# Sort products of the second head pair as two halves of 64 rows, in eights, batched with score units

## The chip, the cores and the metric

The kernel runs on one core of a Trainium2 chip. The core has a matrix engine (TensorE, "PE" in the profile, with its weight loads as "PEld"), a vector engine (VectorE, "DVE"), a scalar engine (ScalarE, "ACT"), a general one (GpSimd, "POOL") and a sync engine that issues DMAs (SyncE, "SP"). The metric is the device time of one execution in microseconds; before the change it was 233.67 (median of three runs, 233.46 to 234.27).

## The reference, cut to what matters

A block-sorted attention over 4 batches, 8 heads, 768 positions and a head dimension of 64, followed by a layer of a mixture-of-experts kind without routing:

```python
P = sort_net                                  # (B, H, 8, 8), five Sinkhorn rounds
k_sorted = einsum('bhij,bhjcd->bhicd', P, k_b)   # blocks of 96 positions, mixed by P
v_sorted = einsum('bhij,bhjcd->bhicd', P, v_b)
scores = scale * q_b @ k_sorted.T             # within each block of 96
attn = softmax(scores)
x = (attn @ v_sorted) as (3072, 512)
h = x @ w_in                                  # 512 -> 2048
out = (h * cos(h)) @ w_out                    # 2048 -> 512
```

## The kernel before

**Staging.** The 3072 rows of the result are worked through in eight *chunks* `n` of 384 rows; chunk `n` is half of batch `n // 2`. A chunk has four *units* `u` of 96 positions (one sorted block) with all 8 heads. For each unit come scores (TensorE into PSUM), maximum and subtraction (VectorE, lines 489 and 491; chunks 0 and 1 lines 781 and 785), an exponential (ScalarE, line 533), a transpose of the weights (by a DMA from the sync queue, line 551, or on TensorE, line 568), `av` (TensorE, line 588), the normalization (VectorE, lines 599 and 601) and a transpose of the result into `xT[n]` (DMA, line 607, or TensorE, line 619). Then the chunk goes through the up layer (line 632: eight steps of eight matmuls of 384 columns, each with a cosine on ScalarE and a product on VectorE) and the down layer (line 657: six half-tiles of eight matmuls of 512 columns).

**Order.** It is written out by hand: engines run their instructions in the order in which the program emits them. `moe_up` and `moe_down` take lists of calls that are emitted between their steps (`slots`) or in the middle of a half-tile (`mid`, `late`). So work of the next chunks (scores, sort products, `av`) stands between the matmuls of the present chunk. The end of the list (from line 1092) is where chunk 1's down layer, chunk 2's up and down layers and so on stand.

**Sort products.** Keys and values are mixed by `P` on TensorE, for a pair of batches at once: the contraction runs over 128 rows, which are 2 batches x 8 heads x 8 blocks, and the moving matrix `bds[1]` (128 x 128) is block-diagonal: rows 0 to 63 (batch 2) have values in columns 0 to 63 only, rows 64 to 127 (batch 3) in columns 64 to 127 only. `k_sort_g` (line 411) does four keys products and copies their 512 columns out with one instruction on ScalarE; `v_sort_g` (line 456) does four or eight values products. 48 key products (`t` from 0) go to `kT2`, 64 value products (`d` from 0) to `vS[1]`. `k_next` and `w_next` take the next four; `w_two` takes eight. After the last key product two DMAs (`k_swap`) exchange halves of the sorted keys.

**Scores.** `scores` (line 436) multiplies 128 rows, of which the 64 of the other head of a pair are zeros in `q_turned`; a unit is 8 such matmuls of 96 columns. `qk_two` (line 498) does two units with the 64 rows that matter alone; the two heads of a pair take different halves of the rows and different PSUM banks. It is used twice, for units (2,2), (2,3) and (5,0), (5,1). `s_ps` (line 754) does units of chunks 0 and 1, chunk 0's in 64 rows by another path (line 764).

**PSUM.** Two pools of slots: `big`, three slots of two banks, and `acc`, two slots of one bank. A tile waits until the last reader of its slot is done.

Of the kernel before, what the change touches and what calls it, by code (L numbers as in the profile page):

```python
# [10 lines left out]
FP32 = mybir.dt.float32  # L11
# [7 lines left out]
def kernel(  # L19
# [112 lines left out]
    def q_of(n, e):  # L132
        return q_turned[n % 2][:, e]
# [277 lines left out]
    def k_sort_g(t0, eng, pool, tag):  # L411
        ps = pool.tile([128, 4, 4 * NB], FP32, name="ks", tag=tag)
        for t in range(4):
            k_products(ps, t, t0 + t, slice(0, 128), bds[1].rearrange("p x i -> p (x i)"),
                       pair)
        copy_on(
            eng, kT2[:, ::2, :, :, t0:t0 + 4].rearrange("p e b m t -> p b e m t"),
            ps.rearrange("p t (b e m) -> p b e m t", b=2, e=2))
# [9 lines left out]
    def keys_of(n, u, h2, hp):  # L428
        g, b2, ih = where(n)
        z = slice(hp, hp + 2)  # L430
        m = h2 * nb + ih * IC + u
        if n < 2:
            return kT[0][:, z, m]
        return kT[1][:, z, m] if g == 0 else kT2[:, z, b2, m]
# [6 lines left out]
    def v_cols(d, permuted, m=128):  # L441
        return vperm[:, d * blk:d * blk + m] if permuted else vv[:, d]
# [13 lines left out]
    def v_sort_g(d0, nd, eng, pool, tag):  # L456
        ps = pool.tile([128, nd, 4 * NB], FP32, name="vs", tag=tag)
        for t in range(nd):
            m = 128 if t < nd - 1 else blk
            nc.tensor.matmul(  # L460
                ps[:m, t], v_cols(d0 + t, True, m), bds[1].rearrange("p x i -> p (x i)"),
                start=True, stop=True)
        copy_on(eng, vS[1][:, :, d0:d0 + nd], ps[:blk].rearrange("p t n -> p n t"))
# [21 lines left out]
    def qk_reduce(n, u, part, sc):  # L485
        w = len(part)
        scv = sc[:blk].rearrange("p e (h c) -> p (e h) c", c=128)[:, :, :blk]
        mx = small.tile([blk, w * H2], FP32, name="mx", tag="mx")
        nc.vector.reduce_max(mx[:], scv, axis=AX.X)  # L489
        s = s_t[n, u][:, part[0]:part[0] + w].rearrange("p e h c -> p (e h) c")  # L490
        nc.vector.tensor_tensor(s, scv, mx.to_broadcast(list(s.shape)), op=ALU.subtract)  # L491

    def qk(n, u):

        s_t[n, u] = sp.tile([blk, 2, H2, blk], FP32, name="s", tag="s")
        qk_part(n, u, [0, 1], big, "big")

    def qk_two(n, u0, u1):

        us = (u0, u1)  # L500
        tiles = [big.tile([128, 2, 512], FP32, name="sc", tag="big") for u in us]
        for u, sc in zip(us, tiles):
            for h2 in range(H2):
                x = (u * H2 + h2) * blk
                for hp in range(2):
                    rows = slice(hp * D, (hp + 1) * D)
                    nc.tensor.matmul(
                        sc[:, hp, h2 * 128:h2 * 128 + blk], q_of(n, hp)[rows, x:x + 128],
                        keys_of(n, u, h2, hp)[rows], start=True, stop=True)
        for u, sc in zip(us, tiles):  # L510
            s_t[n, u] = sp.tile([blk, 2, H2, blk], FP32, name="s", tag="s")
            qk_reduce(n, u, [0, 1], sc)

    def qk_av(n, u, m, *zs):

# [12 lines left out]
    def expo(n, u, on_pe=False):  # L528
        p = p_bufs[cnt[0] % NP]
        cnt[0] += 1  # L530


        nc.scalar.activation(  # L533
            p[:, :, :blk], s_t.pop((n, u)).rearrange("p e h c -> p (e h) c"), AF.Exp,
            scale=scale)
        if u == 0 and n in (NQ, NQ + 1):

            w = 2 * H2 * blk
            c = 2 * (QZ + D) + (n - NQ) * w
            t = kbuf[:, c:c + w].rearrange("p (a c) -> p a c", c=blk)  # L540
        elif n < LATE:
            t = ptp.tile([128, 2 * H2, blk], BF16, name="pT", tag="pT")
        else:

            z, w = (n * IC + u) % 8, 2 * H2 * blk
            t = vperm[:, z * w:(z + 1) * w].rearrange("p (a c) -> p a c", c=blk)
        pT[n, u] = t
        if on_pe:
            pb[n, u] = p
        else:  # L550
            nc.sync.dma_start_transpose(out=t[:], in_=p.rearrange("p a c -> p (a c)"))
# [12 lines left out]
    def p_transpose(n, u, eng, pool, tag):  # L564
        p = pb.pop((n, u))
        ps = pool.tile([128, 2 * H2, 128], BF16, name="pps", tag=tag)
        for a in range(2 * H2):
            nc.tensor.transpose(ps[:blk, a, :blk], p[:, a, :blk], ident[:blk, :blk])
        copy_on(eng, pT[n, u][:blk], ps[:blk, :, :blk])
# [82 lines left out]
    def down(n, ts, half, stores, mid=(), late=()):  # L652
        if half == 0:
            out_ps[ts] = acc.tile([128, Dm], FP32, name="o", tag="acc")
        o = out_ps[ts]
        for f in range(half * FC // 2, (half + 1) * FC // 2):
            nc.tensor.matmul(  # L657
                o[:], gt[n, f // 4][:, f % 4, ts * 128:(ts + 1) * 128], w_out_t[:, f, :],
                start=(f == 0), stop=(f == FC - 1))
            if f % (FC // 2) == FC // 4 - 1:  # L660
                step(mid)
            if f % (FC // 2) == FC // 4:
                step(late)
        if half == 0:
            return
        if stores is None:

            z = (n % 2 * 3 + ts) * 2 * Dm
            o_s = vbuf[:, z:z + 2 * Dm].bitcast(FP32)
        else:  # L670
            o_s = op.tile([128, Dm], FP32, name="o_s", tag="o_s")
        late = n > 0 and ts == TC // 128 - 1
        copy_on(V if late else A, o_s[:], o[:])
        if stores is None or stores == "held":
            kept[n, ts] = o_s
        else:
            store(n, ts, o_s, nc.sync if late else stores)
# [10 lines left out]
    def moe_down(n, slots=(), stores=nc.sync, mid={}, late=()):  # L688

        for e in range(2 * TC // 128):  # L690
            last = e == 2 * TC // 128 - 1
            down(n, e // 2, e % 2, stores, mid.get(e, ()), late if last else ())
            step(slots[e] if e < len(slots) else ())
# [60 lines left out]
    def s_ps(n, u, fill=0):  # L754
        o = ps["s", n, u] = big.tile([128, 2, 512], FP32, name="sc", tag="big")
        keep_warm(fill, o[:, 0])
        if n == 0:
            for a in range(2 * H2):
                hp, c = a // H2, (u * H2 + a % H2) * blk
                for x in range(2):  # L760
                    rows = slice(x * D, (x + 1) * D)
                    m, w = a % H2 * nb + u, HT if a % H2 == H2 - 1 else 64
                    keys = kT[0][rows, 2 * hp].rearrange("p m t -> p (m t)")
                    nc.tensor.matmul(
                        o[:, x, a * HT:a * HT + w], q_of(0, hp)[rows, c:c + 128],
                        keys[:, m * HT:m * HT + w], start=True, stop=True)
            return
        for h2 in range(H2):
            for hp in range(2):
                scores(o[:, hp, h2 * 128:h2 * 128 + blk], n, u, h2, hp)  # L770
# [77 lines left out]
        copy_on(eng, o_s[:], out_ps[ts][:])  # L848
        store(0, ts, o_s)

    wz = iter(range(0, D, 4))
    kz = iter(range(6, 12))

    def k_next():
# [1 line left out]

    def w_next(eng=A, pool=None, tag="acc"):
        v_sort_g(next(wz), 4, eng, pool or acc, tag)

    def w_two(eng=A):  # L860
        v_sort_g(next(wz), 8, eng, *B)
        next(wz)

    kp(2, *B)
    kp(0, *B)
# [226 lines left out]
    expo(2, 0)  # L1092
    expo(2, 1)
    down(1, 0, 0, nc.sync)
    qk_two(2, 2, 3)
    down(1, 0, 1, "held", mid=[(k_sort_g, 0, A, *C)])
    expo(2, 2)
    let_go(1, 0)
    k_sort_g(4, A, *B)
    down(1, 1, 0, nc.sync)  # L1100
    k_sort_g(8, A, *B)
    av(2, 0, True)
    qk(3, 0)
    k_sort_g(16, A, *B)
    expo(2, 3, True)
    down(1, 1, 1, nc.sync)
    k_sort_g(12, A, *B)
    p_hold(2, 2)
    for z in range(3, 6):
        load_pair(vbuf, vin_d, z * CD // 6, (z + 1) * CD // 6)  # L1110
    load_q(4)
    expo(3, 0)
    v_permute(slice(0, 128))
    av(2, 1, True)
    p_transpose(2, 3, A, *C)
    down(1, 2, 0, nc.sync)
    av(2, 2, True)
    x_transpose(2, 1, V, *B)
# [9 lines left out]

    expo(3, 1)
    expo(3, 2)  # L1130
    moe_down(2, [[(qk, 3, 3), (ones, 1), (w_two,)],
                 [(w_two,), (expo, 3, 3), (av, 3, 0)],
                 [(p_hold, 3, 3), (load_q, 5), (w_two,), (qk_av, 4, 0, 3, 1)],
                 [(w_two,)],
                 [(w_two,), (expo, 4, 0), (sine_next,)]],
             mid={3: [(av, 3, 2, True)], 4: [(av, 3, 3, True)], 5: [(x_transpose, 3, 2, V, *B, 3)]})
    q_transpose_dma(5)
    hold(q_turned[1])
# [4 lines left out]
               [(qk_half, 4, 2, 1)], [(qk, 4, 3)]])  # L1143
    expo(4, 1)
    expo(4, 2)
    moe_down(3, [[(expo, 4, 3), (av, 4, 0)], [(qk_two, 5, 0, 1)], [],
                 [(expo, 5, 0)],
                 [(av, 4, 3, True), (expo, 5, 1), (sine_next,)]],
             None, mid={3: [(av, 4, 1)], 4: [(av, 4, 2, True)]},
# [71 lines left out]
```

## Time and profile before

| | us |
|---|---|
| median of three runs | 233.67 |
| the profiled execution | 233.72 |
| its span, first to last instruction | 231.7 |
| TensorE busy | 224.7 |
| VectorE busy | 170.8 |
| ScalarE busy | 154.4 |
| GpSimd busy | 95.9 |

The stages that the diff touches, by the start of their first matmul of the up or down layer: chunk 1's units at 39.4, chunk 1's down layer from 70.2 to 85.3, chunk 2's down layer from 97.9 to 112.7.

How to read it: a line of the timeline has the start, the time from there to the end of the last instruction of the group, the engine, the line of the program and the tiles (output, then inputs), the shape and the count. TensorE's matmuls are pipelined, so the groups overlap by the length of a pipeline; the distance from one group's start to the next one's is what the group holds the engine for. A wait that stands in a view under "PEld" is the wait of a weight load, which may lie beside a matmul that still runs.

### The profile page before, as it was taken

How to read it: one execution, taken by the hardware profiler on the slowest of the kernel's cores; microseconds unless marked ns; L12 is line 12 of the kernel's file. 1: busy time of each engine (PE TensorE's matmuls, PEld its weight loads, DVE VectorE, ACT ScalarE, POOL GpSimd, SP SyncE). 2: the span in 40 equal slices, each digit the busy share in tenths (PEclk: the TensorE clock that was granted, in tenths of full speed). 3: DMA queues.
4: the chain of work that ended last, by engine and by line, in shares of the span. 5: the costliest groups of instructions: out<-in, count | busy, mean ns of one | idle time of the engine just before them, and what ended most of it. 6: DMA issues, size and time to landing. Idle time of an engine off the chain costs nothing.

```text
span 231.7 us, 5423 instructions
## 1 busy us (share of the span) xinstructions
PE 224.7 (97%) x2212; PEld 141.4 (61%) x2212; DVE 170.8 (74%) x291; ACT 154.4 (67%) x209; POOL 95.9 (41%) x121
## 2 busy tenths in 40 slices
PE   8889999999999999999999999999999999999994
PEld 3478899567665666656666456555665566556553
DVE  6769967978789857876489986997699769745700
ACT  5659877767789758795788566746675666716521
POOL 7999999399950186962708101800000000000000
PEclk9999999999999999999999999999999999999999
DMA  5999999994999899878979949954923450351012
GB/s 68 233 188 207 203 207 232 200 222 141 123 134 178 129 170 157 152 171 132 136 134 103 122 79 164 205 83 91 197 101 68 84 173 0 71 143 45 3 45 91
DMA packets 67672, 31.19 MB, mean 135 GB/s; under 512 B 56384, under 2 KB 63168, under 8 KB 67392
## 3 DMA queue, kind: packets, MB, share of 16 engines
q0 software_dynamic: 24048, 13.64, 43.5%
q1 hardware_dynamic: 43312, 17.02, 35.6%
q8 instruction: 17, 0.28, 0.5%
q10 hardware_dynamic: 288, 0.20, 0.3%
q14 instruction: 7, 0.06, 0.1%
HBM read 27.27 MB, written 6.29 MB: 145 GB/s over the span
## 4 chain that ended last, share of the span: by engine, by line
PE 85%; DVE 6%; POOL 2%; DMA 2%; ACT 1%; issue 1%; SPq 0%; POOLq 0%; ACTq 0%
PE h L632 30%; PE o L657 29%; PE h L817 5%; PE o L838 4%; PE sc L438 4%; PE av L588 3%; PE ks L408 2%; DVE s L785 2%; PE vs L460 2%; DVE mx L781 2%; PE o L1185 2%; DMA kTs<-kTs 1%; POOL w_in_t L160 1%; DMA P<-in_sort_net_dram 1%; PE xps L619 1%
## 5 line engine op out<-in xcount | busy, mean ns | idle before, releaser
L632 PE MATMUL h<-xT,w_in_t 128*128 128x384 bf16 x448 | 78.4, 326 | 0.0
L657 PE MATMUL o<-w_out_t,gg 128*128 128x512 bf16 x320 | 76.3, 379 | 0.0
L640 DVE TENSOR_TENSOR gg<-c,h 128x768 bf16<-128x768 f32 x56 | 52.7, 949 | 19.7 <-ACT c L636 19.7
L636 ACT ACTIVATE c<-h,half_pi 128x768 f32<-128x768 f32 x56 | 50.4, 900 | 25.1 <-PE h L632 24.2
L632 PEld LDWEIGHTS <-w_in_t 128*128 128x128 bf16 x448 | 42.3, 98 | 26.3 <-DVE xT L259 0.3
L657 PEld LDWEIGHTS <-gg 128*128 128x128 bf16 x320 | 29.0, 99 | 28.0
L533 ACT ACTIVATE p_buf<-s 96x768 bf16<-96x768 f32 x32 | 26.6, 842 | 5.3 <-DVE s L491 4.0
L179 POOL COPY vperm<-kv 64x768 bf16<-64x768 bf16 (+2 forms) x12 | 28.4, 2422 | 4.1 <-DMA kv<-in_v_dram 4.1
L491 DVE TENSOR_TENSOR s<-sc,mx 96x384 f32<-96x384 f32 (+1 forms) x33 | 24.3, 736 | 1.6
L489 DVE TENSOR_REDUCE mx<-sc 96x4 f32<-96x384 f32 (+1 forms) x33 | 24.0, 728 | 0.0
L601 DVE TENSOR_TENSOR xn<-av,r 96x512 bf16<-96x512 f32 x32 | 22.0, 687 | 1.1
L129 POOL DMA_DIRECT2D kv<-in_q_dram x24 | 16.0, 681 | 0.8 <-issue 0.5
L257 ACT CAST kTs<-ks 128x512 bf16<-128x512 f32 x20 | 11.3, 582 | 5.9 <-PE ks L408 5.0
L257 ACT COPY kv<-o 128x512 f32<-128x512 f32 (+2 forms) x10 | 5.2, 523 | 14.1 <-PE o L657 11.5
L599 DVE RECIPROCAL r<-av 96x8 f32<-96x8 f32 x32 | 6.4, 199 | 10.5 <-PE av L588 9.9
L438 PE MATMUL sc<-kTs,q_turned 128*128 128x96 bf16 x192 | 13.4, 206 | 0.3 <-DMA kTs<-kTs 0.3
L438 PEld LDWEIGHTS <-q_turned 128*128 128x128 bf16 x192 | 10.9, 98 | 3.2 <-issue 0.4
L129 POOL DMA_DIRECT2D q_mem<-in_q_dram x16 | 10.7, 689 | 2.9 <-DMA kv<-in_v_dram 2.5
L838 PE MATMUL o<-w_out_t,gg 128*128 128x512 bf16 x48 | 11.7, 379 | 0.0
L259 DVE COPY kv<-o 128x512 f32<-128x512 f32 (+1 forms) x5 | 3.1, 612 | 11.1 <-PE o L1185 8.5
L817 PE MATMUL h<-xT,w_in_t 128*128 128x192 bf16 x128 | 11.1, 246 | 0.0
L817 PEld LDWEIGHTS <-w_in_t 128*128 128x128 bf16 x128 | 10.5, 98 | 0.0
(130 smaller groups left out, 279.8 us busy)
## 6 DMA issues: line engine op xcount, KB each, us to landing
out_dram<-kv SPq DMA_DIRECT2D x12, 256.0 KB, 2.7
out_dram<-o_s SPq DMA_DIRECT2D x10, 256.0 KB, 3.4
w_in_t<-in_moe_w_in_dram POOLq DMA_DIRECT2D x4, 512.0 KB, 11.7
w_out_t<-in_moe_w_out_dram POOLq DMA_DIRECT2D x4, 512.0 KB, 12.3
kv<-in_k_dram POOLq DMA_DIRECT2D x2, 768.0 KB, 10.1
kv<-in_v_dram POOLq DMA_DIRECT2D x2, 768.0 KB, 13.1
pair<-in_k_dram POOLq DMA_DIRECT2D x2, 768.0 KB, 12.3
kv<-in_v_dram POOLq DMA_DIRECT2D x6, 256.0 KB, 6.2
```

Source lines behind the costliest of these rows:

```text
L129: nc.gpsimd.dma_start(out=q_heads[:, i, :, e], in_=src[:, ih * IC + i, :, e])
L179: nc.gpsimd.tensor_copy(dst, src)
L438: nc.tensor.matmul(out, q_of(n, hp)[:, x:x + 128], keys_of(n, u, h2, hp), start=True, stop=True)
L489: nc.vector.reduce_max(mx[:], scv, axis=AX.X)
L491: nc.vector.tensor_tensor(s, scv, mx.to_broadcast(list(s.shape)), op=ALU.subtract)
L533: nc.scalar.activation(p[:, :, :blk], s_t.pop((n, u)).rearrange("p e h c -> p (e h) c"), AF.Exp, scale=scale)
L601: nc.vector.tensor_tensor(xn.rearrange("p h e d -> p e h d"), avv[:, :, :, :D], r.to_broadcast([blk, 2, H2, D]), op=ALU.mult)
L632: nc.tensor.matmul(h[:, f2, :w], w_in_t[:, kk, f * 128:(f + 1) * 128], xT[n][:, kk], start=(kk == 0), stop=(kk == KC - 1))
L636: nc.scalar.activation(c[:], h[:, :, :w], AF.Sin, bias=half_pi[:, 0:1])
L640: nc.vector.tensor_tensor(gt[n, fp // 2][:, f:f + 2], c[:], h[:, :, :w], op=ALU.mult)
L657: nc.tensor.matmul(o[:], gt[n, f // 4][:, f % 4, ts * 128:(ts + 1) * 128], w_out_t[:, f, :], start=(f == 0), stop=(f == FC - 1))
L817: nc.tensor.matmul(o[:, part, f2 * w:(f2 + 1) * w], w_in_t[:, kk, f * 128:(f + 1) * 128], xT[0][:, kk, h * w:(h + 1) * w], start=(kk == 0) ...
```

## The change

- `qk_two` goes; `by_half` does one unit's scores in 64 rows, and `sort_eight` does eight sort products as 16 matmuls of 64 rows and 64 columns, one for each batch, into the two banks of a `big` slot. `place_eight` copies their 1024 columns out with one instruction.
- `batch` takes a list of such parts, allocates their slots, emits all their matmuls one after the other, and then their reductions and copies.
- In chunk 1's down layer the first eight key products join units (2,2) and (2,3), and the second eight join unit (3,0), behind the layer's fourth half-tile; the group of `t` from 16 and the exponential of (2,3) go into that half-tile, and the exponential of (3,0) moves behind the transposes of (2,3).
- In chunk 2's down layer the five eights of value products (`d` from 0 to 39) become such eights: with unit (3,3), alone, with unit (4,0), alone, alone. `av` of (3,1), which stood behind the products and unit (4,0), is now ahead of them.
- Units (1,0) and (1,1) are done in 64 rows. Units (5,0) and (5,1) stay in 64 rows, through `batch`.

```diff
+    def by_half(n, u, sc):
+
+        for h2 in range(H2):
+            x = (u * H2 + h2) * blk
+            for hp in range(2):
+                rows = slice(hp * D, (hp + 1) * D)
+                nc.tensor.matmul(
+                    sc[:, hp, h2 * 128:h2 * 128 + blk], q_of(n, hp)[rows, x:x + 128],
+                    keys_of(n, u, h2, hp)[rows], start=True, stop=True)
+
+    def sort_eight(kind, z, ps):
+
+        for t in range(8):
+            for b in range(2):
+                rows = slice(b * 64, (b + 1) * 64)
+                if kind == "ks":
+                    m, cols = 128, pair[rows, (z * 8 + t) * 2 * D:(z * 8 + t + 1) * 2 * D]
+                else:
+                    m = 128 if t < 7 else blk
+                    cols = v_cols(z * 8 + t, True, m)[rows]
+                nc.tensor.matmul(
+                    ps[:m, b, t * 2 * NB:(t + 1) * 2 * NB], cols,
+                    bds[1][rows, b * H:(b + 1) * H].rearrange("p x i -> p (x i)"),
+                    start=True, stop=True)
+
+    def place_eight(kind, z, ps, eng):
+        if kind == "ks":
+            copy_on(
+                eng, kT2[:, ::2, :, :, z * 8:z * 8 + 8].rearrange("p e b m t -> p b e m t"),
+                ps.rearrange("p b (t e m) -> p b e m t", t=8, e=2))
+        else:
+            copy_on(
+                eng, vS[1][:, :, z * 8:z * 8 + 8].rearrange("p (b n) d -> p b n d", b=2),
+                ps[:blk].rearrange("p b (t n) -> p b n t", t=8))
+
+    def batch(*parts, between=()):
+
+        tiles = []
+        for kind, *x in parts:
+            ps = big.tile([128, 2, 512], FP32, name=kind, tag="big")
+            tiles.append(ps)
+            if kind == "sc":
+                by_half(*x, ps)
+            else:
+                sort_eight(kind, x[0], ps)
+        step(between)
+        for (kind, *x), ps in zip(parts, tiles):
+            if kind == "sc":
+                s_t[tuple(x)] = sp.tile([blk, 2, H2, blk], FP32, name="s", tag="s")
+                qk_reduce(*x, [0, 1], ps)
+            else:
+                place_eight(kind, *x[:1], ps, x[1])
...
+        if u < 2:
+            by_half(n, u, o)
+            return
...
-    qk_two(2, 2, 3)
-    down(1, 0, 1, "held", mid=[(k_sort_g, 0, A, *C)])
+    batch(("sc", 2, 2), ("sc", 2, 3), ("ks", 0, A))
+    down(1, 0, 1, "held")
     expo(2, 2)
     let_go(1, 0)
-    k_sort_g(4, A, *B)
     down(1, 1, 0, nc.sync)
-    k_sort_g(8, A, *B)
     av(2, 0, True)
-    qk(3, 0)
-    k_sort_g(16, A, *B)
-    expo(2, 3, True)
-    down(1, 1, 1, nc.sync)
-    k_sort_g(12, A, *B)
+    down(1, 1, 1, nc.sync, mid=[(k_sort_g, 16, A, *B), (expo, 2, 3, True)])
+    batch(("sc", 3, 0), ("ks", 1, A))
...
-    expo(3, 0)
     v_permute(slice(0, 128))
     av(2, 1, True)
     p_transpose(2, 3, A, *C)
+    expo(3, 0)
     down(1, 2, 0, nc.sync)
...
-    moe_down(2, [[(qk, 3, 3), (ones, 1), (w_two,)],
-                 [(w_two,), (expo, 3, 3), (av, 3, 0)],
-                 [(p_hold, 3, 3), (load_q, 5), (w_two,), (qk_av, 4, 0, 3, 1)],
-                 [(w_two,)],
-                 [(w_two,), (expo, 4, 0), (sine_next,)]],
+    moe_down(2, [[(ones, 1), (batch, ("sc", 3, 3), ("vs", 0, A))],
+                 [(batch, ("vs", 1, A)), (expo, 3, 3), (av, 3, 0)],
+                 [(p_hold, 3, 3), (load_q, 5), (av, 3, 1),
+                  (batch, ("vs", 2, A), ("sc", 4, 0))],
+                 [(batch, ("vs", 3, A))], [(batch, ("vs", 4, A)), (expo, 4, 0), (sine_next,)]],
              mid={3: [(av, 3, 2, True)], 4: [(av, 3, 3, True)], 5: [(x_transpose, 3, 2, V, *B, 3)]})
```

More of the change, by code (lines that the diff above doesn't have):

```diff
@@ L496, in qk @@
         qk_part(n, u, [0, 1], big, "big")
[L498 to L512, printed above, removed]
+    def by_half(n, u, sc):
[6 more added lines that the diff above has]
+                    keys_of(n, u, h2, hp)[rows], start=True, stop=True)
@@ L849, in down_out @@
         store(0, ts, o_s)
-    wz = iter(range(0, D, 4))
+    wz = iter(range(40, D, 4))
     kz = iter(range(6, 12))
@@ L858, in w_next @@
         v_sort_g(next(wz), 4, eng, pool or acc, tag)
-    def w_two(eng=A):
-        v_sort_g(next(wz), 8, eng, *B)
-        next(wz)
     kp(2, *B)
@@ L1145 @@
     expo(4, 2)
-    moe_down(3, [[(expo, 4, 3), (av, 4, 0)], [(qk_two, 5, 0, 1)], [],
+    moe_down(3, [[(expo, 4, 3), (av, 4, 0)], [(batch, ("sc", 5, 0), ("sc", 5, 1))], [],
                  [(expo, 5, 0)],
```

## The prediction

> **What bounds the kernel now.** I read the page first, then TensorE's timeline through the stretches that the diff touches, then what TensorE waits for, and last the queues that feed those waits.
>
> ```profile
> span 231.7 us, 5423 instructions
> PE 224.7 (97%) x2212; PEld 141.4 (61%) x2212; DVE 170.8 (74%) x291; ACT 154.4 (67%) x209; POOL 95.9 (41%) x121
> PEclk9999999999999999999999999999999999999999
> PE 85%; DVE 6%; POOL 2%; DMA 2%; ACT 1%; issue 1%; SPq 0%; POOLq 0%; ACTq 0%
> ```
>
> TensorE sets the time: it is 85% of the chain that ended last, and its clock is full in every slice. So a matmul saved shortens the kernel, unless the time goes into a wait for VectorE or for a DMA. The profiled run took 233.72 us, 2.0 more than its span, and the runs' median is 233.67; I make the sum against 233.72. A measurement of this kernel can tell about 0.3%, 0.7 us, from no change.
>
> Busy times overlap here, so I price a group of matmuls by its own start and the start of the next group.
>
> ```profile
> 15.69 0.40 PE L764 MATMUL sc<-kTs,q_turned 64*128 64x64 bf16 x16
> 16.02 0.42 PE L745 MATMUL vs<-bdv,vperm 128*128 128x64 bf16 x8
> 39.41 0.84 PE L438 MATMUL sc<-kTs,q_turned 128*128 128x96 bf16 x16
> 40.09 0.38 PE L838 MATMUL o<-w_out_t,gg 128*128 128x512 bf16 x1
> 70.20 1.89 PE L657 MATMUL o<-w_out_t,gg 128*128 128x512 bf16 x8
> 72.02 0.51 PE L507 MATMUL sc<-kTs,q_turned 64*128 64x96 bf16 x16
> 72.47 1.04 PE L657 MATMUL o<-w_out_t,gg 128*128 128x512 bf16 x4
> 73.34 0.39 PE L408 MATMUL ks<-bd,pair 128*128 128x128 bf16 x4
> 73.57 1.03 PE L657 MATMUL o<-w_out_t,gg 128*128 128x512 bf16 x4
> ```
>
> Units in full rows: two (16 matmuls) take 40.09 - 39.41 = 0.68, so one takes 0.34. A sort product in full rows: four take 73.57 - 73.34 = 0.23, and eight of the same kind 100.37 - 99.93 = 0.44 (rows of part (c)): 0.056 each, 0.45 an eight. A 512-column matmul of the down layer: (73.34 - 72.47) / 4 = 0.216.
>
> In 64 rows, two units took 72.47 - 72.02 = 0.45, and the eight matmuls ahead took 1.82 instead of 8 x 0.216 = 1.73: the way in costs 0.10. Sixteen products of 64 columns in 64 rows (eight pairs) took 16.02 - 15.69 = 0.33, way out included. If way in and way out cost about 0.10 each, a pair of 96 columns costs (0.45 - 0.10) / 8 = 0.043 and a pair of 64 columns (0.33 - 0.10) / 8 = 0.029. So **an excursion into 64 rows costs 0.21**, a unit then 0.17 instead of 0.34, an eight of sort products 0.23 instead of 0.45.
>
> **The change part by part.** (a) *Chunk 1's first two units*, adjacent on TensorE: 0.21 + 2 x 0.17 = 0.55 for 0.68. Gain 0.13. VectorE and ScalarE have the same work; TensorE waits for neither there.
>
> (b) *First down layer (chunk 1).* The first eight of key products joins the pair of units that is in 64 rows already: it adds 0.23 and removes two groups of 0.22. Gain 0.21. Unit (3,0) with the second eight: 0.21 + 0.17 + 0.23 = 0.61 for 0.34 + 0.45. Gain 0.17. Two waits go with the old order:
>
> ```profile
> 76.60 0.42 PE L588 MATMUL av<-vS,pT 96*128 96x65 bf16 x8
> 77.00 0.50 PE L438 MATMUL sc<-kTs,q_turned 128*128 128x96 bf16 x8
> 77.44 0.38 PE L408 MATMUL ks<-bd,pair 128*128 128x128 bf16 x4
> 79.61 0.42 PE L588 MATMUL av<-vS,pT 96*128 96x65 bf16 x8
> 79.87 0.54 PE L568 MATMUL pps<-ident,p_buf 96*96 96x96 bf16 x8
> 77.91 0.94 DVE L489 TENSOR_REDUCE mx<-sc 96x8 f32<-96x768 f32 x1
> 78.96 0.95 DVE L491 TENSOR_TENSOR s<-sc,mx 96x768 f32<-96x768 f32 x1
> 80.31 0.69 DVE L601 TENSOR_TENSOR xn<-av,r 96x512 bf16<-96x512 f32 x1
> 83.77 0.69 DVE L601 TENSOR_TENSOR xn<-av,r 96x512 bf16<-96x512 f32 x1
> 84.51 0.34 PE xps L619 x4
> 85.34 0.33 PE L632 MATMUL h<-xT,w_in_t 128*128 128x384 bf16 x1
> 73.31 3.92 SPq L551 DMA_TRANSPOSE pT<-p_buf  x3
> DMA to landing us min/median/max: 3.0/4.1/4.8
> ```
>
> The av group before unit (3,0) held TensorE 0.40, the same group at 79.61 only 0.26: 0.14 of waiting for a slot. The unit took 0.44 instead of 0.34: 0.10 for the next slot. In the new order four matmuls, a group of sort products and four more stand between, so both go. TensorE alone would gain 0.13 + 0.38 + 0.24 = 0.75 up to 79.61.
>
> That is not what arrives at the end of the layer. Unit (3,0) now comes about 1.5 us later, and VectorE works in order: its maximum and subtraction (2.0 from 77.91 to the end of the subtraction with its pause), then three normalizations of about 0.92 with a copy of 0.3 between, 5.0 in all, before the last transposes, which already waited for that normalization (ends 84.46; transposes at 84.51). With TensorE at unit (3,0) from 78.5, its scores are readable at about 78.9 and the last normalization ends at 83.9 to 84.0: 0.5 earlier than now. The second of the three DMA transposes, issued at about 74.6, lands 3.0 to 4.8 later, 77.6 to 79.4, and its av now wants it at 79.0: if it is late, 0.3 more is lost. So I take **0.45 at the end of this layer**, chunk 1's 0.13 included (bounds 0.25 and 0.75). ScalarE's copies of 1024 columns, 1.02 each by the rows of part (c), replace two of half the size; the first delays unit (2,2)'s exponential by half of that, 0.5, so that its transpose, issued at about 75.9 now, lands at 79.4 to 81.2, and it is wanted at 81.5. The exponential of (3,0) moves behind that of the transposed copy; its DMA is read 20 us later, at 102.55. On SP's and POOL's queues nothing else changes place.
>
> (c) *Second down layer (chunk 2).*
>
> ```profile
> 99.59 0.50 PE L438 MATMUL sc<-kTs,q_turned 128*128 128x96 bf16 x8
> 99.93 0.61 PE L460 MATMUL vs<-bd,vperm 128*128 128x128 bf16 x8
> 100.37 1.89 PE L657 MATMUL o<-w_out_t,gg 128*128 128x512 bf16 x8
> 102.55 0.42 PE L588 MATMUL av<-vS,kv 96*128 96x65 bf16 x8
> 102.80 1.89 PE L657 MATMUL o<-w_out_t,gg 128*128 128x512 bf16 x8
> 104.98 0.50 PE L438 MATMUL sc<-kTs,q_turned 128*128 128x96 bf16 x8
> 105.32 0.42 PE L588 MATMUL av<-vS,pT 96*128 96x65 bf16 x8
> 105.58 1.03 PE L657 MATMUL o<-w_out_t,gg 128*128 128x512 bf16 x4
> 106.59 0.43 PE L588 MATMUL av<-vS,pT 96*128 96x65 bf16 x8
> PEld L588 <- DMA pT<-p_buf: 0.5, 1, 0.5
> 101.14 2.56 SPq L551 DMA_TRANSPOSE pT<-p_buf  x2
> DMA to landing us min/median/max: 2.8/3.0/4.1
> 103.13 1.02 ACT L257 CAST pair<-vs 96x1024 bf16<-96x1024 f32 x1
> 104.04 0.85 ACT L533 ACTIVATE p_buf<-s 96x768 bf16<-96x768 f32 x1
> ```
>
> A unit with an eight takes 0.78 now (99.59 to 100.37) and 0.61 then: 0.17, twice. An eight alone takes 0.45 now and 0.21 + 0.23 = 0.44 then, and its last product loads 96 columns, for which I add 0.02: three times 0.01 lost. The copies behind them keep their size and order.
>
> A wait also goes: the four matmuls from 105.58 took 1.01 instead of 0.87, for the transposed weights of unit (3,2). That is 0.14 of TensorE's time (the 0.5 of the waits row is the weight load's, mostly under a matmul). With 0.45 from before and one 0.17 the two transposes are issued 0.45 earlier, and unit (3,2)'s av comes at about 106.1, 4.1 after its issue: free of waiting.
>
> A wait may come in its place: av of (3,1) now stands *ahead* of eight and unit, 0.79 sooner than it did in the order. TensorE reaches it at 104.53 - 0.45 - 0.16 = 103.92. Its transpose is issued at 100.69 and lands after 2.8 to 4.1, at 103.5 to 104.8: nothing or 0.9 lost, and vs, unit (4,0) and their readers stand behind it. By the median of 3.0 it is there at 103.7; I take nothing. Sum of the layer: 2 x 0.17 - 0.03 + 0.14 = **0.45**.
>
> (d) The pair of units (5,0), (5,1) is the same work under another name: nothing.
>
> [...]
>
> Sum: 0.45 + 0.45 = 0.90, of which I leave 0.03 for the semaphores of 56 more matmuls. 233.72 - 0.87 = **232.85**.
>
> **Rivals.** *The gain is swallowed by the next wait* (0.32): av of (3,1) waits half of the possible 0.9, 0.45. For it: three waits on exactly these chains are in the profile. Against: the median landing. 0.87 - 0.45 = 0.42 gained: 233.3. The first layer at its lower bound of 0.25 with the second whole gives nearly the same, 0.25 + 0.45 - 0.03 = 0.67 or 233.05, and both together 233.5.
>
> *Slower by a late transpose* (0.10): av of (3,1) waits for a landing as late as the 4.8 of the first layer, 105.5. TensorE, there at 103.92, loses 1.57, ahead of everything: with 0.61 gained before and 0.29 after, 0.67 lost, 234.4. It decides from a landing at about 104.8; one of the six such transposes of these two layers took 4.8. Against: that one shared its queue with two more and a store.
>
> *The two halves don't run side by side* (0.05), so the change doesn't do what it says: 16 products of 64 columns at 0.029 each make 0.46 an eight, all 1.6 are lost and 234.5 comes out. Against it: the row at 15.69.
>
> *Reading the products out becomes the bound* (0.05): ScalarE goes without a pause from 103.13 to 104.89, and a batch needs two or three of the three slots at once. If the eight at 104.1 found its slot 0.5 late, 233.35. Against: the copy at 103.13 ends at 104.15, 0.45 earlier in the new order, and the eight comes at 104.3. [...]
>
> **How the numbers follow.** The forecast has 0.48, with 232.5 (TensorE's 0.75 and 0.45 in full) to 233.1 for itself. About four fifths of it lie below 232.97, the bound of faster; with a little from the rivals that is 0.41. Slower is the late transpose and the halves above 234.4, half of each, and nearly as much for a cost of the same size that I can't see: 0.14. The rest, 0.45, is within 0.3%. The range goes from 232.3 to 234.1: it leaves out the worst landings and most of the serial halves.
>
> **What would show it.** Right: eights 0.23 apart from their ways in and out, one L-row of 16 for each; the av before unit (3,0) at 0.26; TensorE's first matmul of chunk 2's up layer near 84.9 (85.34 now); chunk 3's 0.9 earlier than now. Wrong: matmuls of 64 rows that start 0.03 apart one by one; an av group of (3,1) with a wait for its DMA ahead of it; more than 0.05 between TensorE's groups after 113, where I expect only the shift.

## The result and the profile after

The changed kernel takes 235.12 us (median of 14 runs, 234.51 to 235.97) against 233.70 before (14 runs, 233.29 to 235.30). The ratio is 1.0051 (95%: 1.0034 to 1.0068): slower by half a percent, where 232.85 and a gain were forecast. The ratios, here and below, leave out the few slow executions (237.03 to 239.18, all but one at a granted clock of 0.993) and are not quotients of the medians, from which they differ by up to 0.2%. The profiled run took 234.85 with a span of 233.1; the spans differ by 1.36, the medians by 1.42.

The page of the changed kernel, its busy times, the chain of waits and the instruction queue:

```profile
span 233.1 us, 5534 instructions
PE 223.4 (96%) x2268; PEld 139.0 (60%) x2268; DVE 170.9 (73%) x291; ACT 154.1 (66%) x207; POOL 96.0 (41%) x121
q8 instruction: 18, 0.29, 0.5%
PE 81%; DMA 6%; DVE 5%; ACT 3%; POOL 2%; issue 1%; SPq 0%; ACTq 0%; POOLq 0%
```

q8 is a DMA queue that the page names "instruction"; its row gives packets, MB and share. TensorE is busy for 1.3 less, as the change intends. Its share of the chain fell from 85% to 81%, and DMA's rose from 2% to 6%. The timeline of TensorE through the two down layers shows where:

```profile
39.46 0.51 PE L504 MATMUL sc<-kTs,q_turned 64*128 64x96 bf16 x16
39.91 0.82 PE L878 MATMUL o<-w_out_t,gg 128*128 128x512 bf16 x3
...
72.08 0.40 PE L518 MATMUL ks<-bd,pair 64*128 64x64 bf16 x16
72.41 3.63 PE L694 MATMUL o<-w_out_t,gg 128*128 128x512 bf16 x16
77.22 0.43 PE L625 MATMUL av<-vS,pT 96*128 96x65 bf16 x8 [1.19 <-DMA pT<-p_buf]
...
79.54 0.34 PE L504 MATMUL sc<-kTs,q_turned 64*128 64x96 bf16 x8
79.72 0.40 PE L518 MATMUL ks<-bd,pair 64*128 64x64 bf16 x16
80.05 0.43 PE L625 MATMUL av<-vS,pT 96*128 96x65 bf16 x8
...
102.49 0.42 PE L518 MATMUL vs<-bd,vperm 64*128 64x64 bf16 x16
102.84 0.43 PE L625 MATMUL av<-vS,kv 96*128 96x65 bf16 x8
103.11 1.90 PE L694 MATMUL o<-w_out_t,gg 128*128 128x512 bf16 x8
106.18 0.43 PE L625 MATMUL av<-vS,pT 96*128 96x65 bf16 x8 [1.17 <-DMA pT<-p_buf]
106.54 0.42 PE L518 MATMUL vs<-bd,vperm 64*128 64x64 bf16 x16
106.80 0.34 PE L504 MATMUL sc<-kTs,q_turned 64*128 64x96 bf16 x8
107.07 1.04 PE L694 MATMUL o<-w_out_t,gg 128*128 128x512 bf16 x4
```

The prices hold: a lone eight 102.84 - 102.49 = 0.35, an eight with a unit 80.05 - 79.54 = 0.51 and 107.07 - 106.54 = 0.53; with the 0.10 that the way in costs the matmul ahead, 0.45 and 0.61 to 0.63 against 0.44 and 0.61 forecast. But av of (2,0) and av of (3,1) each wait for their transposed weights. From the last matmul ahead of them, at 75.65 and 104.63, they start 1.57 and 1.55 later instead of 0.22: 1.35 and 1.34 lost.

The sum closes. Chunk 1's down layer starts 0.30 earlier (69.90 for 70.20), chunk 2's up layer 0.44 later (85.78 for 85.34), chunk 3's 1.37 later (114.04 for 112.67); from there on both kernels take 119.0. So the first down layer lost 0.74 and the second 0.92, and with 1.35 and 1.34 of waiting taken out they would have gained 0.61 and 0.42.

Below are the landings of the two transposes, and the packets of the instruction queue near them, from the trace's DMA records. Each of these packets has 16,384 bytes; the kernel before has 17 of them.

```
            pT (2,0)              pT (3,1)              instruction packets
            issued  landed  lat   issued  landed  lat   start + length
before       73.31   76.27  2.95  101.14  103.96  2.81  64.01+1.25  77.04+1.00  91.80+1.08  103.41+1.44
after        73.04   77.17  4.13  101.59  106.13  4.54  64.32+0.97  74.46+1.01  90.35+1.51  103.13+1.23
```

In the view by windows the last column is what the DMA engines move, in GB/s; a packet counts where it starts. First the changed kernel around the packet at 74.46, then the kernel before around the one at 77.04:

```profile
74.00:74.50 0.50, 0.50 (x4) 0.22 (x3) 0.50 (x1) 0.50 (x1) 0.00 (x0) 1.00 1.29 281
74.50:75.00 0.50, 0.50 (x4) 0.20 (x2) 0.50 (x2) 0.50 (x2) 0.00 (x0) 1.00 2.42 176
75.00:75.50 0.50, 0.50 (x4) 0.26 (x3) 0.50 (x1) 0.50 (x2) 0.00 (x0) 1.00 1.89 21
75.50:76.00 0.50, 0.50 (x3) 0.04 (x1) 0.40 (x2) 0.38 (x1) 0.00 (x0) 1.00 0.08 9
76.00:76.50 0.50, 0.03 (x1) 0.00 (x0) 0.50 (x1) 0.00 (x0) 0.00 (x0) 1.00 0.62 126
```

```profile
77.00:77.50 0.50, 0.50 (x11) 0.45 (x10) 0.40 (x2) 0.39 (x1) 0.00 (x0) 1.00 3.35 121
77.50:78.00 0.50, 0.50 (x6) 0.36 (x6) 0.50 (x2) 0.08 (x1) 0.00 (x0) 1.00 0.81 6
78.00:78.50 0.50, 0.50 (x4) 0.20 (x2) 0.50 (x1) 0.50 (x2) 0.00 (x0) 1.00 0.09 9
78.50:79.00 0.50, 0.50 (x4) 0.24 (x3) 0.40 (x2) 0.50 (x2) 0.00 (x0) 1.00 0.58 120
```

The 281 is mostly an earlier transpose of queries; that of (2,0) moves in the second window, at 176 GB/s. From 0.5 to 0.6 behind the start of the instruction packet until 0.7 behind its end hardly a packet of the transposes starts any more: 21 and 9 GB/s after, 6 and 9 before. Before, that fell on the transposes of (2,1) and (2,2); now it falls on that of (2,0), the first one that TensorE needs.

The theory that I went on to test, **T**: TensorE's instructions come in blocks of 16,384 bytes over the same DMA engines as the transposes (the page counts the packets of both in the time of the same 16 engines), one for some 250 to 260 of them (18 for 4,536 recorded matmuls and weight loads, 17 for 4,424); a transpose that is under way then lands some 1.3 later, an estimate from the two landings (4.13 for 2.95 and 4.54 for 2.81 after the issue) and the two waits (1.35 and 1.34). The change adds 56 matmuls with their weight loads, so blocks come earlier, and it brings the readers forward: av of (2,0) from 76.60 to 75.87, av of (3,1) ahead of an eight and a unit. No row says whose instructions a block holds; the packets of the other instruction queue of the page, q14, are 7 in both kernels. The rival, **R**: the order alone does it, readers that come too early, and the landings have no part in it.

### The profile page after: what moved, and what is told of

It is laid out like the page before. It is cut to its first block, busy times and chain, and to the rows that moved or that the text cites. A ratio compares the mean times of both kernels' runs of the same rounds, so it can differ in the third digit from the quotient of the medians.

```text
span 233.1 us, 5534 instructions
## 1 busy us (share of the span) xinstructions
PE 223.4 (96%) x2268; PEld 139.0 (60%) x2268; DVE 170.9 (73%) x291; ACT 154.1 (66%) x207; POOL 96.0 (41%) x121
## 4 chain that ended last, share of the span: by engine, by line
PE 81%; DMA 6%; DVE 5%; ACT 3%; POOL 2%; issue 1%; SPq 0%; ACTq 0%; POOLq 0%
PE h L669 30%; PE o L694 26%; PE h L857 5%; PE o L878 4%; DMA pT<-p_buf 4%; PE av L625 3%; PE sc L438 3%; PE ks L408 2%; DVE s L825 2%; DVE mx L821 2%; PE o L1216 2%; DMA kTs<-kTs 1%; PE xps L656 1%; ACT p_buf L570 1%; PE sc L504 1%
## 5 line engine op out<-in xcount | busy, mean ns | idle before, releaser
L669 PEld LDWEIGHTS <-w_in_t 128*128 128x128 bf16 x448 | 42.3, 98 | 26.3 <-issue 0.5
L257 ACT CAST kTs<-ks 128x512 bf16<-128x512 f32 (+1 forms) x18 | 11.0, 631 | 7.6 <-PE ks L408 6.7
L438 PE MATMUL sc<-kTs,q_turned 128*128 128x96 bf16 x152 | 11.0, 206 | 0.2 <-DMA kTs<-kTs 0.2
L257 ACT CAST pair<-vs 96x512 bf16<-96x512 f32 (+1 forms) x11 | 8.6, 780 | 3.0 <-PE vs L518 3.0
```

Source lines behind the costliest of these rows:

```text
L257: eng.copy(dst, src)
L669: nc.tensor.matmul(h[:, f2, :w], w_in_t[:, kk, f * 128:(f + 1) * 128], xT[n][:, kk], start=(kk == 0), stop=(kk == KC - 1))
```

## The experiments

All medians stand beside those of the kernel before in the same job: 233.83 for the first four kernels, 233.67 for the next four, 233.51 for the last.

**One reader back.** av of (3,1) goes behind the batch that it had been put ahead of.

```diff
-                 [(p_hold, 3, 3), (load_q, 5), (av, 3, 1),
-                  (batch, ("vs", 2, A), ("sc", 4, 0))],
+                 [(p_hold, 3, 3), (load_q, 5),
+                  (batch, ("vs", 2, A), ("sc", 4, 0)), (av, 3, 1)],
```

> The changed kernel with av of unit (3,1) put back behind the third eight of values and unit (4,0). Theory T (the two DMA transposes that TensorE waits for land late because a 16 KB block of TensorE's own instructions is fetched over the same DMA engines while they run; the change moved these fetches and moved the readers forward): the transpose of (3,1) lands as late as now, about 4.5 us after its issue, at 106.1; the eight and the unit cover 0.6 of the wait, 0.7 of 1.34 stays, span 232.5. Rival R (order alone: the landings are what they were before the change, only the readers come too early): the transpose lands 2.8 after its issue, no wait for (3,1) at all, span 231.8. In both the wait of 1.35 ahead of av of (2,0) stays.

Measured: 234.06, ratio 1.0009 (0.9989 to 1.0028), span 232.2. On TensorE's timeline:

```profile
105.17 0.42 PE L518 MATMUL vs<-bd,vperm 64*128 64x64 bf16 x16
105.43 0.33 PE L504 MATMUL sc<-kTs,q_turned 64*128 64x96 bf16 x8
105.97 0.43 PE L625 MATMUL av<-vS,pT 96*128 96x65 bf16 x8 [0.20 <-DMA pT<-p_buf]
```

The landing stays late (issued 101.82, landed 105.92: 4.10), the wait shrinks from 1.34 to about 0.3 (105.97 - 105.43 = 0.54, where unit and way out took 0.27 above, 106.80 to 107.07), and the second down layer takes 14.66 (before 14.81, changed 15.73). The wait of av (2,0) stays. The span lies between T's 232.5 and R's 231.8; the landing is T's. So the position decides how much of a late landing is paid, and the landing is late all the same.

**Half of the change.** The first down layer as it was before; chunk 1's units and the second layer as changed.

```diff
-    batch(("sc", 2, 2), ("sc", 2, 3), ("ks", 0, A))
-    down(1, 0, 1, "held")
+    batch(("sc", 2, 2), ("sc", 2, 3))
+    down(1, 0, 1, "held", mid=[(k_sort_g, 0, A, *C)])
...
```

> The changed kernel with chunk 1's down layer in its old order and its key products in 128 rows (the pair of units (2,2), (2,3) in 64 rows as before). R: the first wait (1.35) goes, the second (1.34) stays, since the order of the second layer is the same; the first layer ends 0.3 earlier than in the kernel before (chunk 1's gain), span near 232.4. T: the first layer has 32 instructions less, so the fetch of 103.13 comes 32 instructions later in the program, after the transpose of (3,1) has run: that wait falls below 0.5 and the wait of (3,2) may take over up to 0.5; span 231.3 to 231.9.

Measured: 234.49, ratio 1.0016 (0.9986 to 1.0046), span 232.5. The block is fetched at 76.66, pT (2,0) lands 2.94 after its issue, and its av doesn't wait; the first layer takes 15.14, as before. pT (3,1) lands 4.56 after its issue, with a block at 103.25, and its av waits 1.35 as in the changed kernel. T's guess at where that block would fall was wrong, and the span is the one that R gave. The runs lie in two groups: five from 233.25 to 233.75, seven from 234.38 to 235.44 (the profiled one, 235.14, is of these). It may be that the same program meets the late landing in some executions and not in others; the lower group has no trace.

**More instructions, nothing else.** The idle matmuls at the start, which only keep TensorE busy, are cut narrower: in the kernel before 24 more matmuls (48 instructions). In the changed kernel fills of 512 columns that stand later are cut in four as well, and it is 66 more (132); the first part below is in the changed kernel alone.

```diff
     def keep_warm(times, t, cols=512):
+        if cols == 512:
+            times, cols = times * 4, 128
...
-    keep_warm(14, big.tile([128, 512], FP32, name="idle", tag="big"))
+    keep_warm(38, big.tile([128, 512], FP32, name="idle", tag="big"), 188)
```

> The changed kernel with the warm-up matmuls of chunk 0 cut into narrower ones of the same width in all: 66 more matmuls, 132 more TensorE instructions ahead of everything that the change touches, nothing else. T: the block fetched at 74.46 comes some 132 instructions sooner, near 69, the one at 103.13 near 99, both before the transposes of (2,0) and (3,1) are under way; these land 3.0 after their issue (near 76.0 and 104.5), the waits of 1.35 and 1.34 shrink to 0.2 each, span near 230.9. R: the landings and waits stay, span 233.1.

> The kernel before with the first 14 warm-up matmuls cut into 38 narrower ones: 48 more TensorE instructions ahead, nothing of the change. T: the fetch of 77.04 comes near 74.7, in the transposes ahead of (2,0)'s, which then lands about 0.9 later (77.2 instead of 76.3), and av of (2,0), due at 76.6, waits some 0.6; part of it is taken up by the waits behind it; span 231.9 to 232.3. The other fetch, 103.41, comes near 100.8, and the wait of (3,2) goes (0.15). R: no landing changes, span 231.7.

Measured in the changed kernel: 235.54, ratio 1.0052 (1.0018 to 1.0086), span 232.9. In the kernel before: 235.31, ratio 1.0058 (1.0030 to 1.0086), span 233.5. Two things happen in each. First, the transpose of (2,0) does what T says. In the changed kernel the blocks come at 73.04 and 95.55 (T had guessed 69 and 99), pT (2,0), issued behind the first, lands 2.80 after its issue and its av no longer waits; chunk 1's down layer takes 14.53. Chunk 2's still takes 15.36: pT (3,1) lands 3.64 after its issue with no block over it, which T doesn't explain, and its av waits 0.43; a third transpose, with a block over it, lands 4.49 after its issue. In the kernel before the block moves from 77.04 to 75.07, from 3.7 behind the issue of pT (2,0) to 0.9 behind it; the transpose lands 3.87 after its issue for 2.95, and its av waits 0.62 for it where it waited for no landing:

```profile
78.04 0.43 PE L588 MATMUL av<-vS,pT 96*128 96x65 bf16 x8 [0.46 <-DMA pT<-p_buf]
```

R, by which nothing changes, is refuted. Second, neither theory had foreseen the start: the first block now comes at 13.33 instead of 15.97 in the changed kernel and at 12.70 instead of 16.22 in that of before, upon the first load of the values. GpSimd's copy of them, on the timelines of the changed kernel with the cut and of the kernel before:

```profile
15.44 1.47 POOL L179 COPY vperm<-kv 64x768 bf16<-64x768 bf16 x1 [1.71 <-DMA kv<-in_v_dram]
```

```profile
14.11 2.93 POOL L179 COPY vperm<-kv 64x768 bf16<-64x768 bf16 x2 [0.36 <-DMA kv<-in_v_dram]
```

The same load lands 1.3 later (15.39 and 15.38 for 14.05) in both kernels, and all layers come later from the first on: chunk 0's down layer at 40.96 for 39.91 in the changed kernel, at 41.02 for 40.09 in that of before. That the block makes the load late is likely, not shown: no run has a block upon that load without this edit. So the medians of these two kernels say nothing on T; the landings do.

**More instructions, behind that load.** The changed kernel, order and all; idle matmuls of 512 and 256 columns that fill pauses between 20 and 26 us are cut into ones of 64, 33 more.

```diff
-        keep_warm(fill, a[:, 0], 256)
+        keep_warm(fill * 4, a[:, 0], 64)
...
-        keep_warm(fill, o.rearrange("p t n -> p (t n)"))
+        keep_warm(fill * 8, o.rearrange("p t n -> p (t n)"), 64)
```

> The changed kernel as it is, order and all, with 33 more matmuls on TensorE between 20 and 26 us, where idle 512- and 256-column matmuls that only fill a pause are cut into ones of 64 columns (same total time). Theory T: 66 more instructions bring each later block's fetch forward, from 74.4 to about 72, from 90.4 to about 86.5, from 103.1 to about 100.6, off the transposes of (2,0) and (3,1): pT of (2,0) lands 2.8 to 3.0 after its issue, that of (3,1) 2.8 to 3.6, their av wait 0.1 and 0.3 at most, other transposes may be hit later; span 230.4 to 231.2 although the kernel does more, time about 232.6. Rival (the order alone, readers too early): both waits of 1.35 stay, span 233.1.

Measured: 234.86, ratio 1.0044 (1.0021 to 1.0067), span 232.3. Its timeline, in an order that is the changed kernel's word for word, and a row of what TensorE waits for late in the kernel:

```profile
74.66 1.46 PE L694 MATMUL o<-w_out_t,gg 128*128 128x512 bf16 x5
76.02 0.43 PE L625 MATMUL av<-vS,pT 96*128 96x65 bf16 x8
...
102.57 1.24 PE L694 MATMUL o<-w_out_t,gg 128*128 128x512 bf16 x5
103.65 0.42 PE L625 MATMUL av<-vS,pT 96*128 96x65 bf16 x8
```

```profile
PE h L669 <- DMA xT<-xn: 1.1, 1, 1.1
```

Both waits of 1.35 are gone. The blocks come at 73.33, 86.55, 97.80 and 108.76; the first one begins 0.23 after the issue of pT (2,0), and ends at 74.39, as its data begins to move (74.3). The two transposes land 2.88 and 3.17 after their issue, the layers take 14.60 and 14.39, and chunk 3's up layer starts at 111.50, 2.54 ahead of the changed kernel. R is refuted here too. By the end two thirds of that lead are gone again, 1.3 of the 1.7 in the stretch before the last up layer: a later block, at 202.73, comes there, and the layer waits 1.1 for its transposed input (the row above). The span is 1.1 to 1.9 above T's figure; T had named such later hits without a price for them. In the other runs, most of them longer than the profiled one, more must be lost; they have no trace.

**Chunk 1 alone.** The kernel before with units (1,0) and (1,1) in 64 rows: as many instructions as before.

```diff
+                if u < 2:
+                    rows = slice(hp * D, (hp + 1) * D)
...
+                    nc.tensor.matmul(o[:, hp, h2 * 128:h2 * 128 + blk], q_of(n, hp)[rows, x:x + 128],
+                        keys_of(n, u, h2, hp)[rows], start=True, stop=True)
+                    continue
                 scores(o[:, hp, h2 * 128:h2 * 128 + blk], n, u, h2, hp)
```

> The kernel before with chunk 1's units (1,0) and (1,1) in 64 rows and nothing else; the number of TensorE's instructions is that of before. Theory T: blocks are fetched at the same instructions, transposes land as before, and 0.13 by its matmuls, up to 0.3 as the changed kernel showed at 69.9, arrives at the end: span 231.4 to 231.6, time 233.4 to 233.6. Rival (the first gain is lost again in a wait): 231.7.

Measured: 233.69, ratio 1.0008 (0.9976 to 1.0040). Eight of its twelve runs lie from 233.21 to 233.73; the profiled one, of 235.20 and a span of 233.3, isn't among them, and so it shows what such an execution contains. The av of (2,0) on the timeline, and the windows ahead of it:

```profile
78.28 0.43 PE L588 MATMUL av<-vS,pT 96*128 96x65 bf16 x8 [1.78 <-DMA pT<-p_buf]
```

```profile
76.00:76.50 0.50, 0.50 (x6) 0.21 (x3) 0.50 (x1) 0.16 (x1) 0.00 (x0) 1.00 0.92 156
76.50:77.00 0.50, 0.00 (x0) 0.00 (x0) 0.17 (x1) 0.47 (x1) 0.00 (x0) 1.00 4.18 61
77.00:77.50 0.50, 0.00 (x0) 0.00 (x0) 0.00 (x0) 0.12 (x1) 0.00 (x0) 1.00 0.03 3
77.50:78.00 0.50, 0.00 (x0) 0.00 (x0) 0.00 (x0) 0.00 (x0) 0.00 (x0) 1.00 0.08 9
```

The block came at 75.76 and took 1.61, and pT (2,0) landed 4.94 after its issue. T's "at the same instructions" is too strong: with as many instructions as before the block came 1.3 earlier than in the profile of before. In the layer's start the 0.13 arrived (69.93 for 70.20, of which 0.13 is a shorter wait for the sorted keys near 60).

**Both readers back.** The first experiment, and av of (2,0) behind the fifth matmul of the next half-tile.

```diff
-    av(2, 0, True)
-    down(1, 1, 1, nc.sync, mid=[(k_sort_g, 16, A, *B), (expo, 2, 3, True)])
+    down(1, 1, 1, nc.sync, mid=[(k_sort_g, 16, A, *B), (expo, 2, 3, True)],
+         late=[(av, 2, 0, True)])
...
-                 [(p_hold, 3, 3), (load_q, 5), (av, 3, 1),
-                  (batch, ("vs", 2, A), ("sc", 4, 0))],
+                 [(p_hold, 3, 3), (load_q, 5),
+                  (batch, ("vs", 2, A), ("sc", 4, 0)), (av, 3, 1)],
```

> The changed kernel with both readers moved back: av of (3,1) behind the batch of vs 2 and unit (4,0), and av of (2,0) into the second half of the half-tile behind it (after its fifth matmul). Theory T (blocks of TensorE's instructions are fetched at about 74.4 and 103, transposes in flight then land 1.3 later): the landings stay late (pT of (2,0) near 77.3, of (3,1) near 105.5), but av of (2,0) wants its weights only at about 77.2 and waits 0.25 at most; av of (3,1) waits 0.4 at most. Up layer of chunk 2 at 84.6 to 84.9 (85.78 in the changed kernel), span 231.0 to 231.3, time about 233.0. Rival (the change itself costs more than its matmuls, by reading out or semaphores, and the waits only show where): the layers keep 15.9 and 15.7, span 232.5 or more.

Measured: 233.23, ratio 0.9966 (0.9943 to 0.9989), span 231.5: faster than both kernels. The first layer takes 14.52 for 15.14 before, though pT (2,0) lands late (77.28). The second takes 15.41: a block at 102.60 delays the second exchange of the sorted keys (landed 104.56, before 102.87) and, behind it in SP's queue, pT (3,1) (105.25). What TensorE waits for in that layer:

```profile
PE sc L504 <- DMA kTs<-kTs: 0.4, 1, 0.4
PE av L625 <- DMA pT<-p_buf: 0.4, 1, 0.4
```

**Second layer alone, reader back.** Half of the change with the first experiment's edit.

> Chunk 1's two units and the second down layer of the change alone (the first down layer is that of before, unit (3,0) and the key products in 128 rows), with av of (3,1) behind the batch of vs 2 and unit (4,0). Theory T: pT of (3,1) lands near 105.4 as with the first layer old, wanted about 0.8 later than there, so its av waits about 0.5; second down layer 14.9 to 15.1 (15.75 with av ahead), span 231.6. Rival (the order alone makes the wait, the landing is that of before, 2.8 after the issue): no wait, layer 14.4, span 231.2.

Measured: 233.81, ratio 0.9993 (0.9966 to 1.0021). The profiled execution, 233.09 with a span of 231.2, is the shortest of its runs: there pT (3,1) landed 2.81 after its issue with the block at 103.14, its av didn't wait, and the layer took 14.69. That is R's landing and R's span, but the block began 2.39 after the issue, when the transpose's data had passed; in the kernel before it began 2.26 after it, and the landing was on time as well. In half of the change, with the block at 103.25, it was 2.40 after an issue at 100.85 and the landing came at 4.56. The semaphore's updates tell a little more: a transpose has landed with the last of sixteen. In half of the change fourteen had come 2.80 after the issue, and the last two came at 4.55 and 4.56; here all sixteen had come at 2.81. At this edge neither theory tells which it will be.

**Everything late one half-tile later.** On top of both readers back.

```diff
-                  (batch, ("vs", 2, A), ("sc", 4, 0)), (av, 3, 1)],
-                 [(batch, ("vs", 3, A))], [(batch, ("vs", 4, A)), (expo, 4, 0), (sine_next,)]],
-             mid={3: [(av, 3, 2, True)], ...
+                  (batch, ("vs", 2, A))],
+                 [(av, 3, 2, True), (batch, ("vs", 3, A), ("sc", 4, 0))], ...
+             mid={3: [(av, 3, 1)], ...
```

> The kernel with both readers moved back, and in the second down layer everything that needs a late landing one half-tile later: unit (4,0) (which needs the second exchange of the sorted keys) with vs 3 instead of vs 2, av of (3,1) into the fourth half-tile, av of (3,2) behind that. Theory T: the exchange lands near 104.5 and the weights of (3,1) near 105.3 as before this edit, but unit (4,0) wants the one at about 106.5 and av of (3,1) the other at about 104.9: waits 0.5 together at most (1.1 with both readers back alone); second down layer 14.5 to 14.9 (15.4 there), span 230.6 to 231.0, time about 232.6. Rival (unit (4,0) and the normalizations crowd on VectorE, so that the last transposes of the layer are late): layer 15.4 or more, with the waits for VectorE ahead of the transposes.

Measured: 232.82 (232.50 to 233.66), ratio 0.9967 (0.9954 to 0.9980), span 231.8: as good as both readers back and no better. What TensorE waits for in the layer:

```profile
PE av L625 <- DMA pT<-p_buf: 0.4, 1, 0.4
PE h L669 <- DMA xT<-xn: 0.2, 1, 0.2
```

In this execution pT (3,1) landed 5.09 after its issue, and a block at 109.99 made the last transposed result late (4.62, landed 112.71). The layer took 15.36 against 14.5 to 14.9 expected, in an execution of 233.59, among the longest of its twelve; VectorE, the rival's cause, is not what TensorE waited for.

**All executions together.** The eleven traces hold 99 transposes of weights (nine each). Sorted by whether a block's fetch begins less than 2.8 after the issue and ends more than 0.4 after it, bounds that were chosen after the landings were known:

```
                 count   median   lowest   highest
block under way     45     4.09     2.81      5.09    (42 of them 3.46 or more)
no block            54     2.92     2.77      3.92    (51 of them 3.32 or less)
```

Three with a block were on time, at 2.81, 2.81 and 2.88 (two of the edge and the first of the shifted kernel); three without one were late, at 3.46, 3.64 and 3.92.

## Why the prediction was wrong

**The bound and the prices of TensorE were right.** TensorE sets the end (81% of the chain). An excursion into 64 rows costs what was forecast (0.45 for a lone eight, 0.44 forecast; 0.55 for chunk 1's pair, 39.91 - 39.46 and 0.10, as forecast). The halves run side by side (the 16 matmuls of a lone eight in 0.35, where the rival had 0.46), no wait of TensorE in these layers points to the reading of the products, and from 114 on nothing changed. The 0.03 left for semaphores rests on no row, and no run measures it.

**(a) Chunk 1: right.** 0.13 forecast; chunk 1's down layer starts 0.05 to 0.38 earlier in the eight kernels that have the edit and start as before, 0.30 in the changed one; 0.13 of that is a shorter wait for the sorted keys near 60, which wasn't forecast.

**(b) First down layer: the first step that failed is a wait put at nothing, that of av of (2,0); one limit was also mis-sized.** Without the late landing the layer gains 0.54 (14.60 for 15.14) in the shifted kernel, whose order is the changed one's, and 0.62 (14.52) with both readers back, which is TensorE's 0.38 and the two waits' 0.24 in full. The limit by VectorE, "0.5 earlier than now", was 0.24 too strict: with both readers back the last normalization starts at 83.03 and ends at 83.72, not 83.9 to 84.0. The risk was seen for the second transpose, which cost nothing, and for that of (2,2), which cost nothing either. Of the first, pT (2,0), the text says nothing: the av of (2,0) was moved forward by 0.73, to 75.87, and the only landing of before was at 76.27. Issued 0.3 earlier it would have been there at about 76.0 at best, and 4.1 after its issue at 77.1. It landed at 77.17, and 1.35 was lost: the gain became a loss of 0.74.

**(c) Second down layer: the second step that failed is "By the median of 3.0 it is there at 103.7; I take nothing."** The gain of 0.45 was right (0.42 in the shifted kernel). But a median is no price here: most landings come about 2.9 after the issue or about 4.1, by whether a block of instructions is under way. The rows of before, 2.8/3.0/4.1 and 3.0/4.1/4.8, showed both kinds: three of the six were late, not the one of 4.8 alone. Because of the first layer's loss TensorE reached av of (3,1) at 104.85, not at 103.92; the transpose was issued at 101.59 and landed 4.54 later, and 1.34 was lost; the rival had 1.57 for 4.8.

**The rivals.** The late transpose was among them, at 234.4 and one chance in ten, with the right mechanism on TensorE's side, and for (3,1) alone. It came twice over: 231.7 - 0.3 - 0.6 - 0.4 + 1.35 + 1.34 makes the span of 233.1. What made it likely wasn't considered, that added instructions themselves move traffic on the DMA engines (with 48 more a block came at 75.07 for 77.04): the rival's objection, that a landing of 4.8 came of a shared queue, took the cause to be somewhere the change didn't touch. All 14 runs of the changed kernel are above 234.5, which fits late landings in every execution, and 235.3 in one of 14 of the kernel before would fit one there; only one execution of each has a trace.

**What stays open.** What sets the moment of a block's fetch beyond the count of instructions: the same count gave 77.04 in one execution and 75.76 in another kernel's. Why in the second layer a fetch 2.4 after the issue once made two of sixteen updates 1.75 late and once none. And what the executions without a trace met.

## What to carry to other kernels

A matmul split in two costs more than its time on TensorE: here it added instructions (56 matmuls and their weight loads, 18 blocks for 17), and their fetches fell on other transfers, so ask which transfer will be under way when the next block comes. Where the landings of one kind of DMA fall into two groups (here medians of 2.92 and 4.09 after the issue), cost a reader by the late group, and leave it that much room; moving two readers back, by a batch and by five matmuls, turned a loss of 0.5% into a gain of 0.3%. Work saved upstream can also bring readers forward without bringing their transfers forward as much (here av of (2,0) by 0.73 and its transpose by 0.27).

## What the runs showed of the hardware

In the changed kernel the transposes fell from 176 GB/s to 21 and 9 for about a microsecond, from 0.5 behind the start of one packet of 16,384 bytes, 1.01 us long (0.9 to 1.7 in all traces), until 0.7 behind its end. Over all traces the transposes with such a packet over them landed 1.2 later (median 4.09 for 2.92). The first load of the values wasn't stopped in the same way: with a block upon it the total rate stayed about as it was without one (201 and 199 GB/s for 213 and 197), yet that load landed 1.3 later. A block came for every 241 to 249 recorded matmuls and weight loads on average, by run (some records are missing); single intervals went from 159 to 324.
